# Sliding-window attention in three passes over one Trainium2 core: scores of each half tile of queries against its own 192 keys

## Chip, cores and metric

The kernel runs on one core of one Trainium2 chip. The metric is device time in microseconds (us) of one execution; of several executions the median is taken, and lower is better. All inputs lie in device memory when it starts.

## What is computed

Three stages in a row on 4 sequences of 576 tokens: attention of 8 heads of 64 channels with a window of 128 keys, a mixing of tokens with a channel MLP, and a layer norm with a second channel MLP. The change touches the first stage alone:

```python
scores = scale * np.matmul(q, k.transpose(0, 1, 3, 2))       # 4 x 8 x 576 x 576, 64 channels
rel = pos[:, None] - pos[None, :]
mask = (rel >= 0) & (rel < window)                            # window = 128
scores = np.where(mask, scores + bias[None], -1000000000.0)   # bias = -slope(head) * |rel|
attn = np.exp(scores - np.max(scores, axis=-1, keepdims=True))
attn = attn / (np.sum(attn, axis=-1, keepdims=True) + 1e-09)
return np.matmul(attn, v)
```

A query sees itself and the 127 keys before it. The token mixing is `x + (relu(xT w_tok1) w_tok2)T`, the MLPs are `u + relu(u w_ch1) w_ch2`.

## The kernel before

The 2304 tokens are 18 tiles of 128. One sequence is four and a half tiles, so tile 0 and tile 9 begin a sequence and see their own keys alone; the other 16 tiles see their own 128 keys and the 128 of the tile before.

**Attention of a tile** goes through these steps, in two parts c of four heads each. `load_qk` (L527) fetches the tile's keys into one of the four places of `keys` (a ring), and its queries. `scores` (L591) multiplies, for each of the pairs p of heads, the queries of head j (j = 0, 1) with the keys: 64 channels of head j lie on partitions 64 j to 64 j + 63, so the two heads of a pair take one half of TensorE's rows each. The result `ps_s` has 128 queries on the partitions, and for each j a PSUM bank of its own. For a tile with two key tiles these are 256 columns in fp32. In `softmax`, `copy_predicated` (L626) folds them into 128 columns: column k of the own tile is replaced by column k of the tile before where k lies behind the query (`after` is that mask), since of these two keys the window holds exactly one. Then come a DVE instruction for each head that adds the bias and takes the minimum (L632, on the negated scores), an exponential for each head on ACT (L641), four transposes on TensorE into `ps_t` (L648), a copy out of PSUM (L359) and on POOL two selections (L658) that separate own and previous keys again. `values` (L603) multiplies these with `v`, two heads at once on two halves of TensorE's columns. `normalize` copies the sum out (`ut`, L359), transposes it back (L670) and divides (L372).

**Order of the work.** `packed(i, i2)` records the scores of tile i and the values of tile i - 2 as one block on TensorE: two parts of scores, then two of values. All operations are recorded first with a cost for each engine and a list of what they need, and `Plan.order` then puts them in order for every engine by these costs: what is ready and is due first goes first. The order on an engine is fixed when the program is built. So a changed cost or a new operation can also move operations far from it, and some operations may go to DVE or to POOL (the helpers `minus` L372 and `convert_w`), whichever the plan finds sooner free. The token mixing of earlier tiles (`tok1`, L438 to L440, `tok2`, L728 to L730) is filled in between the attention blocks on TensorE; the conversion of the weights from 64-bit floats goes on beside it on DMA, ACT and DVE (L402 to L429). The MLPs follow: `seven_products` (L987 to L989) and `second` (L1042 to L1044) with DVE adding each result to `u` (L1047).

Of the kernel before, what the change touches and what calls it, by code (L numbers as in the profile page):

```python
# [10 lines left out]
F32 = mybir.dt.float32  # L11
# [39 lines left out]
def batches_of(i):  # L51

    out, t, end = [], i * P, (i + 1) * P
    while t < end:
        b, s = divmod(t, S)
        n = min(end - t, S - s)
        out.append((b, t - i * P, n, s))
        t += n
    return out
# [43 lines left out]
class Plan:  # L103
# [22 lines left out]
    def buf(self, pool, shape, dtype, tag, bufs=1):  # L126
        b = Buf(self, pool, shape, dtype, tag, bufs)
        ring = self.rings.setdefault((pool, tag), [])
        if len(ring) >= bufs:
            b.after = [ring[-bufs]]  # L130
        if ring:
            b.behind = ring[-1]
        ring.append(b)
        return b
# [176 lines left out]
def pe(n):  # L311
    return 2.6 + n / 2.4


def block_kernel(tc, qT, kT, v, wt1, wt2, wa1, wa2, wb1, wb2, g, bias, out):
# [5 lines left out]
    def op(cost, emit, reads=(), writes=(), behind=()):  # L321
        return pl.op(cost, (lambda e: emit()) if len(cost) == 1 else emit, reads, writes, behind)
# [192 lines left out]

    bias_sb = buf("att", [P, 4, H, P], BF16, "bias_sb")

    keys = buf("att", [P, RING, H // 2, P], F32, "keys")
    wt1h, wt1l = ([buf("tok", [P, 5, TOK], F32R, f"wt1{x}{odd}") for odd in range(2)] for x in "hl")
    wt2h = buf("tok", [P, 2, S + P], F32R, "wt2h")  # L520
    wt2l = buf("tok", [P, 2, S + P], F32R, "wt2l")
# [2 lines left out]
    def load_qk(i):  # L524
        r = i % RING
        b = qs[i] = buf("att", [P, H // 2, P], F32, "q", Q_BUFS)
        op({"DMA": 1000}, lambda: nc.sync.dma_start(out=keys.t[:, r].rearrange("p h t -> p (h t)"), in_=kT[i]),  # L527
           writes=[(keys, r)])
        load(b, lambda: b.t.rearrange("p h t -> p (h t)"), P * DM * 4, qT[i])

    def load_v(i):
# [25 lines left out]

    def keys_of(i):

        s = i % RING  # L560
        if starts_batch(i):
            return [i], 0, 0, (s, s + 1, 1)
        table = 3 if len(batches_of(i)) > 1 else 2 if len(batches_of(i - 1)) > 1 else 1
        if s == 0:
            return [i, i - 1], 0, table, (0, RING, RING - 1)
        return [i - 1, i], 1, table, (s - 1, s + 1, 1)

    pv = buf("psb", [P, H // 2, P], F32, "ps_v")
    rs_t, xh_t, xl_t = {}, {}, {}
# [3 lines left out]
    def packed(i, i2):  # L573
# [4 lines left out]

        parts, ready = [], []
        if i is not None:  # L580
            tiles, own, table, (a0, a1, a2) = keys_of(i)
            w = len(tiles) * P
            x = qs[i]
            for c in range(2):
                ps_t[i, c] = buf("psa", [P, 2, 2, 2 * P], F32, "ps_s", 2)

                def scores(c=c, ps=ps_t[i, c]):
                    for p in range(2):
                        for j in range(2):
                            r = slice(j * D, (j + 1) * D)  # L590
                            nc.tensor.matmul(ps.t[:, j, p, :w], x.t[r, 2 * c + p], keys.t[r, a0:a1:a2, 2 * c + p],  # L591
                                             start=True, stop=True)

                parts.append((4 * pe(2 * w), scores, [x] + [(keys, t % RING) for t in tiles], [ps_t[i, c]]))
        if i2 is not None:
            tiles2 = keys_of(i2)[0]
            na = len(tiles2)
# [19 lines left out]

    def softmax(i, c):

        tiles, own, table, _ = keys_of(i)  # L620
        na = len(tiles)
        ps = ps_t[i, c]
        o = slice(own * P, (own + 1) * P)
        if na == 2:
            b = slice((1 - own) * P, (2 - own) * P)
            op({"DVE": 690}, lambda: nc.vector.copy_predicated(  # L626
                ps.t[:, :, :, o], after.t.bitcast(I32).unsqueeze(1).unsqueeze(1).to_broadcast([P, 2, 2, P]),
                ps.t[:, :, :, b]), [ps, after], [ps])
        t = buf("att", [P, 4, P], F32, "t", T_BUFS)
        mn = buf("small", [P, 4], F32, "mn", 3)  # L630
        for m in range(4):
# [569 lines left out]
```

## Time and profile before

| | before |
|---|---|
| median of 3 runs (lowest, highest) | 865.22 us (863.85, 865.59) |
| the profiled execution's own time | 863.28 us |
| its span, first to last instruction | 861.6 us |
| instructions in the profile | 13160 |
| TensorE (PE) busy, share of the span | 834.8 us, 97% |
| VectorE (DVE) | 654.0 us, 76% |
| ScalarE (ACT) | 367.7 us, 43% |
| GpSimd (POOL) | 347.6 us, 40% |
| mean granted clock of TensorE | 0.992 |

A matmul's record reaches from its start to the end that is modelled for it, and records overlap, so a busy share of 97% doesn't say that TensorE streams columns all the time. Where the text speaks of the length of a block of matmuls, it takes the time from the block's first start to the first start of the block behind it. An fp32 matmul of the program leaves two records, so the 8 score matmuls of a tile are 16 records and the 16 value matmuls 32.

### The profile page before, as it was taken

What the parts mean: (1) busy time and instruction counts of PE and PEld (TensorE: products, weight loads), DVE (VectorE), ACT (ScalarE), POOL (GpSimd) and SP (SyncE); (2) the same over time, 40 slices, a digit from 0 to 9 for tenths busy, and PEclk for the clock granted to TensorE, in tenths of its full rate; (3) what the DMA queues carried; (4) which work ended last, traced back from release to release, by engine and by line L of the source; (5) the groups of instructions that cost most, each with busy time, mean ns of one, the idle gap of its engine ahead of it and who ended that gap; (6) DMA issues with size and microseconds to landing.
All of it is one profiled execution on the core that took longest, in us unless ns stands there. A gap on an engine that the chain in (4) does not pass through costs nothing.

```text
span 861.6 us, 13160 instructions
## 1 busy us (share of the span) xinstructions
PE 834.8 (97%) x4478; PEld 688.6 (80%) x4478; DVE 654.0 (76%) x1371; ACT 367.7 (43%) x880; POOL 347.6 (40%) x362
## 2 busy tenths in 40 slices
PE   7999999898999999999997999999999999999997
PEld 6777888676888888788886888888888888888886
DVE  5787676979888889978899956879779755555554
ACT  6888765553344535233355322333354322222221
POOL 2685444555343656522245434534145712221110
PEclk9999999989999999999999999999999999999999
DMA  8588534375778799977861521897377762221112
GB/s 294 184 226 259 186 114 148 110 239 157 246 223 275 265 328 319 355 248 250 279 211 37 194 85 64 257 300 233 126 257 216 242 215 74 74 73 49 49 50 97
DMA packets 73123, 163.92 MB, mean 190 GB/s; under 512 B 8289, under 2 KB 8417, under 8 KB 73057
## 3 DMA queue, kind: packets, MB, share of 16 engines
q1 hardware_dynamic: 72576, 161.78, 56.9%
q0 software_dynamic: 480, 1.31, 0.7%
q8 instruction: 35, 0.57, 0.3%
q14 instruction: 32, 0.25, 0.1%
HBM read 130.55 MB, written 31.20 MB: 188 GB/s over the span
## 4 chain that ended last, share of the span: by engine, by line
PE 65%; DVE 8%; DMA 1%; issue 1%; ACT 0%; SPq 0%; DVEq 0%; ACTq 0%
PE acc L1044 12%; PE acc L1042 12%; PE acc L1043 12%; PE b L987 9%; PE b L989 9%; PE b L988 9%; DVE st L833 2%; DVE u L1047 1%; DVE st L372 1%; PE b L438 1%; PE b L440 1%; PE p L841 1%; PE b L439 1%; DVE hl L920 1%; DVE xl L372 1%
## 5 line engine op out<-in xcount | busy, mean ns | idle before, releaser
L1047 DVE TENSOR_TENSOR u<-acc,u 128x512 f32<-128x512 f32 x252 | 172.3, 686 | 63.5 <-PE acc L1044 60.3
L1042 PE MATMUL acc<-w2h,hh 128*128 128x512 f32 x504 | 198.6, 394 | 2.0 <-DVE u L1047 1.3
L1044 PE MATMUL acc<-w2h,hl 128*128 128x512 f32 x504 | 197.1, 391 | 2.7 <-DVE hl L920 2.6
L1043 PE MATMUL acc<-w2l,hh 128*128 128x512 f32 x504 | 196.9, 391 | 0.0
L918 ACT ACTIVATE hh<-b 128x512 fp32r<-128x512 f32 (+1 forms) x140 | 74.5, 553 | 275.3 <-PE b L989 242.2
L989 PE MATMUL b<-xh,w1l 128*128 128x512 f32 x392 | 154.0, 393 | 2.8 <-DVE w1l L372 2.8
L987 PE MATMUL b<-xh,w1h 128*128 128x512 f32 x392 | 154.3, 394 | 2.2 <-DVE hl L920 1.2
L988 PE MATMUL b<-xl,w1h 128*128 128x512 f32 x392 | 153.5, 392 | 0.0
L920 DVE SCALAR_TENSOR_TENSOR hl<-b,hh 128x512 fp32r<-128x512 f32 (+1 forms) x140 | 85.4, 630 | 59.3 <-ACT hh L918 59.1
L372 POOL TENSOR_TENSOR w1l<-w,w1h 128x512 fp32r<-128x512 f32 (+1 forms) x53 | 68.3, 1289 | 148.9 <-ACT w1h L359 148.6
L1044 PEld LDWEIGHTS acc<-w2h,hl 128*128 128x128 f32 x504 | 94.9, 188 | 23.9 <-DVE hl L920 4.0
L1042 PEld LDWEIGHTS acc<-w2h,hh 128*128 128x128 f32 x504 | 95.2, 189 | 22.9 <-DVE u L1047 3.1
L1043 PEld LDWEIGHTS acc<-w2l,hh 128*128 128x128 f32 x504 | 95.1, 189 | 18.6
L372 POOL TENSOR_TENSOR w1l<-st,w1h 128x512 fp32r<-128x512 f32 x37 | 49.8, 1346 | 113.4 <-ACT w1h L359 102.9
L987 PEld LDWEIGHTS b<-xh,w1h 128*128 128x128 f32 x392 | 74.3, 190 | 18.8 <-DVE hl L920 2.0
L989 PEld LDWEIGHTS b<-xh,w1l 128*128 128x128 f32 x392 | 74.3, 189 | 18.8 <-DVE w1l L372 3.3
L988 PEld LDWEIGHTS b<-xl,w1h 128*128 128x128 f32 x392 | 74.2, 189 | 15.3
L414 ACT ACTIVATE e<-rh 128x512 bf16<-128x512 bf16 (+2 forms) x65 | 41.3, 636 | 65.9 <-DMA rh<-wb 39.8
L641 ACT ACTIVATE pr<-t,mn 128x128 f32<-128x128 f32 x144 | 55.9, 392 | 18.5 <-DVE mn L632 18.5
L658 POOL TENSOR_SCALAR_AFFINE_SELECT pf<-pf 128x512 f32<-128x512 f32 x64 | 42.2, 659 | 34.0 <-ACT pf L359 31.5
L372 DVE TENSOR_TENSOR b<-b,p 128x512 f32<-128x512 f32 x56 | 38.9, 695 | 19.5 <-PE b L989 19.2
L372 POOL TENSOR_TENSOR w2l<-w,w2h 128x512 fp32r<-128x512 f32 x23 | 31.1, 1357 | 47.1 <-ACT w2h L359 46.9
(117 smaller groups left out, 1373.0 us busy)
## 6 DMA issues: line engine op xcount, KB each, us to landing
w<-d SPq DMA_DIRECT2D x85, 256.0 KB, 4.1
rw<-wb SPq DMA_DIRECT2D x32, 512.0 KB, 5.0
rh<-wb SPq DMA_DIRECT2D x32, 512.0 KB, 4.4
rw<-wa SPq DMA_DIRECT2D x24, 512.0 KB, 4.2
rh<-wa SPq DMA_DIRECT2D x24, 512.0 KB, 4.6
d<-y SPq DMA_DIRECT2D x29, 256.0 KB, 4.5
keys<-kT SPq DMA_DIRECT2D x18, 256.0 KB, 4.1
q<-qT SPq DMA_DIRECT2D x18, 256.0 KB, 4.5
```

The costliest lines, as they stand in the source:

```text
L372: pl.op({e: cost[e] for e in on}, lambda e: ENGINE[e].tensor_tensor(get(), ga(), gb(), alu), [*several(a), *several(b), *also], several(dst))
L641: op({"ACT": 580}, lambda m=m: nc.scalar.activation(out=pr.t[:, m], in_=t.t[:, m], func=AF.Exp, bias=mn.t[:, m:m + 1], scale=-1.0, accum_o ...
L658: op({"POOL": 630}, lambda a=a: nc.gpsimd.affine_select(pf.t[:, a], pf.t[:, 1], [[0, 4], [1 - 2 * a, P]], (ALU.is_ge, ALU.is_gt)[a], 0.0, ...
L918: op({"ACT": act(n, True)}, lambda: nc.scalar.activation(out=hh.t[:, c], in_=go(), func=AF.Relu), [o], [(hh, key)])
L920: mark[0] = op({"DVE": dve(n)}, lambda: nc.vector.scalar_tensor_tensor(out=hl.t[:, c], in0=go(), scalar=0.0, in1=hh.t[:, c].bitcast(F32), ...
L987: nc.tensor.matmul(g.t, wh.t[:, w], xh.t, start=start and k == 0, stop=False, skip_group_check=True)
L988: nc.tensor.matmul(g.t, wh.t[:, w], xl.t, start=False, stop=False, skip_group_check=True)
L989: nc.tensor.matmul(g.t, wl.t[:, w], xh.t, start=False, stop=stop and k == 1, skip_group_check=True)
L1042: nc.tensor.matmul(o.t, hh.t[:, c:c + P], wh.t, start=j == 0, stop=False)
L1043: nc.tensor.matmul(o.t, hh.t[:, c:c + P], wl.t, start=False, stop=False)
L1044: nc.tensor.matmul(o.t, hl.t[:, c:c + P], wh.t, start=False, stop=j == 1)
L1047: op({"DVE": dve(DM)}, lambda o=o, i=i: nc.vector.tensor_tensor(u[i].t, o.t, u[i].t, ALU.add), [o], [u[i]])
```

## The change

For tiles with two key tiles, each head's score matmul of 128 queries with 256 keys becomes two matmuls: queries 0 to 63 with keys 0 to 191, queries 64 to 127 with keys 64 to 255. Half q of the queries stands on TensorE's columns 64 q to 64 q + 63 and writes partitions 64 q to 64 q + 63 of `ps_s`, so that two heads and two halves of queries take a quarter of TensorE each. A tile that begins a sequence keeps its form.

So that 192 keys lie in one row, `keys` is now laid out with the tiles side by side in five places, and the keys of every fourth tile (place 4) are loaded a second time into place 0, where the next tile finds them in front of its own; four of the 18 tiles are loaded twice.

`copy_predicated` becomes two: columns 64 to 127 of the own tile on all 128 partitions, and columns 0 to 63 on partitions 0 to 63 (queries 64 to 127 need none there). The own keys now always come last. Costs of the plan: a part of the scores counts 661 ns where it counted 864, and a fold twice 430 where it counted 690.

```diff
@@ -515,7 +515,12 @@
 
     bias_sb = buf("att", [P, 4, H, P], BF16, "bias_sb")
 
-    keys = buf("att", [P, RING, H // 2, P], F32, "keys")
+
+    keys = buf("att", [P, H // 2, (RING + 1) * P], F32, "keys")
+
+    def span(r, h, first, n):
+        return keys.t[r, h, first:first + n]
+
     wt1h, wt1l = ([buf("tok", [P, 5, TOK], F32R, f"wt1{x}{odd}") for odd in range(2)] for x in "hl")
     wt2h = buf("tok", [P, 2, S + P], F32R, "wt2h")
     wt2l = buf("tok", [P, 2, S + P], F32R, "wt2l")
@@ -524,8 +529,10 @@
     def load_qk(i):
         r = i % RING
         b = qs[i] = buf("att", [P, H // 2, P], F32, "q", Q_BUFS)
-        op({"DMA": 1000}, lambda: nc.sync.dma_start(out=keys.t[:, r].rearrange("p h t -> p (h t)"), in_=kT[i]),
-           writes=[(keys, r)])
+        for j in (r + 1, 0) if r == RING - 1 else (r + 1,):
+            op({"DMA": 1000}, lambda j=j: nc.sync.dma_start(out=keys.t[:, :, j * P:(j + 1) * P],
+                                                             in_=kT[i].rearrange("p (h t) -> p h t", t=P)),
+               writes=[(keys, j)])
         load(b, lambda: b.t.rearrange("p h t -> p (h t)"), P * DM * 4, qT[i])
 
     def load_v(i):
@@ -557,13 +564,9 @@
 
     def keys_of(i):
 
-        s = i % RING
         if starts_batch(i):
-            return [i], 0, 0, (s, s + 1, 1)
-        table = 3 if len(batches_of(i)) > 1 else 2 if len(batches_of(i - 1)) > 1 else 1
-        if s == 0:
-            return [i, i - 1], 0, table, (0, RING, RING - 1)
-        return [i - 1, i], 1, table, (s - 1, s + 1, 1)
+            return [i], 0
+        return [i - 1, i], 3 if len(batches_of(i)) > 1 else 2 if len(batches_of(i - 1)) > 1 else 1
 
     pv = buf("psb", [P, H // 2, P], F32, "ps_v")
     rs_t, xh_t, xl_t = {}, {}, {}
@@ -578,20 +581,30 @@
 
         parts, ready = [], []
         if i is not None:
-            tiles, own, table, (a0, a1, a2) = keys_of(i)
-            w = len(tiles) * P
+            tiles, table = keys_of(i)
+            a1 = i % RING + 2
+            a0, w = a1 - len(tiles), len(tiles) * P
             x = qs[i]
             for c in range(2):
                 ps_t[i, c] = buf("psa", [P, 2, 2, 2 * P], F32, "ps_s", 2)
 
                 def scores(c=c, ps=ps_t[i, c]):
                     for p in range(2):
-                        for j in range(2):
-                            r = slice(j * D, (j + 1) * D)
-                            nc.tensor.matmul(ps.t[:, j, p, :w], x.t[r, 2 * c + p], keys.t[r, a0:a1:a2, 2 * c + p],
-                                             start=True, stop=True)
-
-                parts.append((4 * pe(2 * w), scores, [x] + [(keys, t % RING) for t in tiles], [ps_t[i, c]]))
+                        if len(tiles) == 1:
+                            for j in range(2):
+                                r = slice(j * D, (j + 1) * D)
+                                nc.tensor.matmul(ps.t[:, j, p, :w], x.t[r, 2 * c + p], span(r, 2 * c + p, a0 * P, w),
+                                                 start=True, stop=True)
+                            continue
+
+                        for q in range(2):
+                            for j in range(2):
+                                r, m = slice(j * D, (j + 1) * D), slice(q * D, (q + 1) * D)
+                                nc.tensor.matmul(ps.t[m, j, p, q * D:q * D + 3 * D], x.t[r, 2 * c + p, m],
+                                                 span(r, 2 * c + p, a0 * P + q * D, 3 * D), start=True, stop=True)
+
+                parts.append((4 * pe(3 * D if w > P else P) * (2 if w > P else 1), scores,
+                              [x] + [(keys, k) for k in range(a0, a1)], [ps_t[i, c]]))
         if i2 is not None:
             tiles2 = keys_of(i2)[0]
             na = len(tiles2)
@@ -617,15 +630,18 @@
 
     def softmax(i, c):
 
-        tiles, own, table, _ = keys_of(i)
+        tiles, table = keys_of(i)
         na = len(tiles)
+        own = na - 1
         ps = ps_t[i, c]
         o = slice(own * P, (own + 1) * P)
         if na == 2:
-            b = slice((1 - own) * P, (2 - own) * P)
-            op({"DVE": 690}, lambda: nc.vector.copy_predicated(
-                ps.t[:, :, :, o], after.t.bitcast(I32).unsqueeze(1).unsqueeze(1).to_broadcast([P, 2, 2, P]),
-                ps.t[:, :, :, b]), [ps, after], [ps])
+
+            for rows, c0 in ((P, D), (D, 0)):
+                op({"DVE": 430}, lambda rows=rows, c0=c0: nc.vector.copy_predicated(
+                    ps.t[:rows, :, :, P + c0:P + c0 + D],
+                    after.t[:rows, c0:c0 + D].bitcast(I32).unsqueeze(1).unsqueeze(1).to_broadcast([rows, 2, 2, D]),
+                    ps.t[:rows, :, :, c0:c0 + D]), [ps, after], [ps])
         t = buf("att", [P, 4, P], F32, "t", T_BUFS)
         mn = buf("small", [P, 4], F32, "mn", 3)
         for m in range(4):
```

**What moves.** On TensorE, around the scores of tile 6 (`ps_s` scores, `ps_v` values and, with `ut`, their transposes back, `ps_t` the transposes of the softmax, `tok` the token mixing), before:

```order
L591 MATMUL ps_s<-keys,q 128x256 x8
L603 MATMUL ps_v<-pf,v 64x128 x16
L648 MATMUL ps_t<-ident,pr 128x128 x4
L670 MATMUL ps_v<-ident,ut 128x128 x4
L438 MATMUL tok<-xh,wt1h_381 128x512
L439 MATMUL tok<-xl,wt1h_381 128x512
L440 MATMUL tok<-xh,wt1l_402 128x512
L648 MATMUL ps_t<-ident,pr 128x128 x4
```

and with the change:

```order
L603 MATMUL ps_s<-keys,q 64x192 x16
L616 MATMUL ps_v<-pf,v 64x128 x16
L664 MATMUL ps_t<-ident,pr 128x128 x4
L686 MATMUL ps_v<-ident,ut 128x128 x4
L664 MATMUL ps_t<-ident,pr 128x128 x4
L438 MATMUL tok<-xh,wt1h_419 128x512
L439 MATMUL tok<-xl,wt1h_419 128x512
L440 MATMUL tok<-xh,wt1l_432 128x512
```

The scores are 16 matmuls where they were 8, and the second four transposes of the softmax stand ahead of the three matmuls of the token mixing that they stood behind; it is so at tile 4 too.

On DVE, the fold of tile 3, both parts, with what follows it, before:

```order
L626 COPY_PREDICATED ps_s<-after,ps_s 128x4x128 x2
L632 ISA t,mn<-ps_s,bias_sb 128x128
L632 ISA mn 128x1
```

and with the change:

```order
L641 COPY_PREDICATED ps_s<-after,ps_s 128x4x64 x2
L641 COPY_PREDICATED ps_s<-after,ps_s 64x4x64 x2
L648 ISA t,mn<-ps_s,bias_sb 128x128
L648 ISA mn 128x1
```

The two large pieces, one of each part, go first and the two small ones behind them, all four ahead of the first bias instruction.

On SyncE, whose queue issues the loads in this order, the first loads of keys, queries and values, before:

```order
L527 DMA keys<-kT 128x512
L351 DMA v<-v 128x512
L351 DMA q<-qT 128x512
L351 DMA v<-v 128x512
L760 DMA bias_sb<-bias 128x2048
L402 DMA rh<-wt 128x2048
L527 DMA keys<-kT 128x512
```

and with the change:

```order
L533 DMA keys<-kT 128x4x128
L351 DMA v<-v 128x512
L351 DMA q<-qT 128x512
L533 DMA keys<-kT 128x4x128
L351 DMA v<-v 128x512
L776 DMA bias_sb<-bias 128x2048
L533 DMA keys<-kT 128x4x128
```

The first row is tile 3 into place 4, the fourth is the same tile into place 0; each load is now written in pieces of 128 elements. In the stages behind, the kinds and numbers of instructions are the same on TensorE and ACT, some transposes of `u` stand some tens of rows further ahead, and of the low parts `w1l` (128x512) of the weights 34 stand on DVE where 27 stood, the others on POOL.

## Rows read from the trace of the kernel before

**Rows 1.** The page's first part, and of the second the granted clock

```profile
span 861.6 us, 13160 instructions
PE 834.8 (97%) x4478; PEld 688.6 (80%) x4478; DVE 654.0 (76%) x1371; ACT 367.7 (43%) x880; POOL 347.6 (40%) x362
PEclk9999999989999999999999999999999999999999
```

**Rows 2.** Stretches: length, busy time by engine (instructions), granted clock, DMA share, GB/s

```profile
0.00:20.00 20.00, 15.12 (x112) 12.19 (x114) 10.48 (x60) 13.60 (x55) 5.07 (x19) 0.97 0.86 303
20.00:82.00 62.00, 60.32 (x569) 46.77 (x567) 47.98 (x216) 53.45 (x198) 41.61 (x62) 0.98 0.76 219
82.00:147.00 65.00, 65.00 (x560) 53.55 (x560) 44.78 (x162) 43.59 (x142) 32.09 (x45) 1.00 0.47 153
147.00:180.00 33.00, 28.64 (x126) 22.87 (x125) 31.42 (x44) 17.70 (x32) 16.89 (x13) 0.90 0.42 132
180.00:862.00 682.00, 665.70 (x3119) 553.24 (x3117) 519.35 (x893) 239.39 (x457) 251.97 (x223) 1.00 0.57 191
```

**Rows 3.** PE in order of time: start, length of the group, line, shape, records

```profile
41.52 2.00 PE L591 MATMUL ps_s<-keys,q 64*128 64x256 f32 x16
43.45 1.97 PE L603 MATMUL ps_v<-pf,v 128*64 128x128 f32 x32
45.35 0.66 PE L648 MATMUL ps_t<-ident,pr 128*128 128x128 f32 x4
46.12 0.66 PE L670 MATMUL ps_v<-ident,ut 128*128 128x128 f32 x4
46.53 0.47 PE L438 MATMUL tok<-xh,wt1h 128*128 128x512 f32 x1
...
47.30 0.60 PE L648 MATMUL ps_t<-ident,pr 128*128 128x128 f32 x4
```

**Rows 4.** PE in order of time, tile 9, which has one key tile

```profile
63.03 1.16 PE L591 MATMUL ps_s<-keys,q 64*128 64x128 f32 x16
64.12 0.33 PE L603 MATMUL ps_v<-pf,v 128*64 128x128 f32 x2
```

**Rows 5.** PE and its weight loads to 145 us, by shape: busy, mean ns of one

```profile
L591 PE MATMUL ps_s<-keys,q 64*128 64x256 f32 x256 | 33.4, 402 | 0.7 <-DMA q<-qT 0.7
L603 PEld LDWEIGHTS ps_v<-pf,v 128*64 128x64 f32 x522 | 28.1, 137 | 5.8 <-issue 2.3 <-POOL pf L658 1.3 <-DVE ps_s L626 1.0
L591 PEld LDWEIGHTS ps_s<-keys,q 64*128 64x128 f32 x288 | 26.5, 194 | 7.1 <-issue 3.0 <-DVE mn L632 1.0 <-DVE m L421 0.2
```

**Rows 6.** PE in order of time, first and last of six score blocks from 81.95 us

```profile
81.95 2.00 PE L591 MATMUL ps_s<-keys,q 64*128 64x256 f32 x16
...
125.69 2.00 PE L591 MATMUL ps_s<-keys,q 64*128 64x256 f32 x16
```

**Rows 7.** DVE to 145 us, by shape: busy, mean ns of one

```profile
L626 DVE COPY_PREDICATED ps_s<-after,ps_s 128x512 f32<-128x512 int32 x32 | 22.1, 695 | 11.5 <-PE ps_s L591 10.8 <-issue 0.6
L429 DVE SCALAR_TENSOR_TENSOR w<-m,s 128x512 f32<-128x512 uint32 x5 | 4.1, 824 | 0.0
L429 DVE SCALAR_TENSOR_TENSOR y<-m,s 128x256 f32<-128x256 uint32 x5 | 2.1, 425 | 0.2
```

**Rows 8.** PE in order of time, the first blocks and tile 8's exponentials

```profile
7.38 2.00 PE L591 MATMUL ps_s<-keys,q 64*128 64x256 f32 x16 [0.70 <-DMA q<-qT]
...
61.62 1.47 PE L648 MATMUL ps_t<-ident,pr 128*128 128x128 f32 x4
```

**Rows 9.** ACT between 41 and 48 us, in order of time

```profile
45.47 0.60 ACT L359 ACTIVATE ut<-ps_v 128x512 f32<-128x512 f32 x1 [0.41 <-PE ps_v L603]
46.10 0.60 ACT L359 ACTIVATE pf<-ps_t 128x512 f32<-128x512 f32 x1
```

**Rows 10.** The page's DMA part: the hardware queue, and the keys' loads

```profile
q1 hardware_dynamic: 72576, 161.78, 56.9%
...
keys<-kT SPq DMA_DIRECT2D x18, 256.0 KB, 4.1
```

**Rows 11.** PE where the MLP begins

```profile
170.23 0.40 PE L988 MATMUL b<-xl,w1h 128*128 128x512 f32 x1
173.45 0.80 PE L989 MATMUL b<-xh,w1l 128*128 128x512 f32 x1 [2.82 <-DVE w1l L372]
174.04 0.63 PE L987 MATMUL b<-xh,w1h 128*128 128x512 f32 x1
```

## The prediction

> **What bounds the kernel now.** I read the page's busy shares first, then the stretches, then TensorE in order of time around one attention tile, then DVE's and ACT's rows for the steps between. TensorE is busy 97% of the span at full clock [rows 1], but its records overlap, so the stretches have to say where it really sets the pace [rows 2]. The attention lies in the first 147 us. From 0 to 20 us TensorE is busy 15.12 of 20: the start is a chain of loads, softmax steps and transposes. From 20 to 82 us it is busy 60.32 of 62, with ACT close behind at 53.45. From 82 to 147 us it is busy 65.00 of 65, with DVE at 44.78 and ACT at 43.59: here TensorE is the bound and nothing else is near. From 147 to 180 us DVE is the tight one (31.42 of 33). So a shorter block on TensorE counts in full from 82 to 147 us, partly from 20 to 82, and hardly before 20.
>
> **The score block.** In tile 6 the scores start at 41.52 and the values behind them at 43.45, so a block of 16 records takes 1.93 us [rows 3]. Sixteen records of 0.402 us each make 6.4 us, which do not fit in 1.93 one after the other [rows 5]: the two heads of a pair run side by side, in 8 steps of two. Tile 9 has the same 16 records with 128 columns and takes 64.12 - 63.03 = 1.09 us [rows 4]. The difference, 0.84 us, is 8 steps times 128 columns, so 128 columns cost 0.105 us a step, and 1.93 - 8 x 0.21 = 0.25 us is fixed (first weights, last results, change to the next form). The value block, 32 records, takes 45.35 - 43.45 = 1.90 us, in 16 steps of two halves of TensorE's columns, so halves by columns run side by side as well as halves by rows [rows 3].
>
> The change makes 16 matmuls of 192 columns, 32 records. If four quarters run side by side these are 8 steps of 0.1575 us: 1.26 + 0.25 = 1.51 us, a gain of 0.42. A weight load of 64 columns takes 137 ns where one of 128 takes 194 [rows 5], and the first load of a block is not hidden, which gives up to 0.05 more. **I take 0.45 us a block**; there are 16 such blocks. No row shows four quarters at once, so the bounds are wide. Best: 0.47. Middle: records that cannot follow each other faster than in the value block, (1.90 - 0.25) / 32 = 0.052 us, make 1.90 us, a gain of 0.03. Worst: only two quarters at a time, 16 steps of 0.1575 + 0.25 = 2.77 us, a loss of 0.84. I take the good end, because rows and columns each already run in pairs, and because in both pair forms the step is what its columns need (16 steps of 0.105 and 0.25 make 1.93 for the value block, which takes 1.90).
>
> The Trainium skill, "TensorE: Matmul & The Clock Gate", section "Wait — 56ns, not 53.3ns?", speaks against the change: with hardware decode off, the sequencer spends about 62 ns on each matmul, and that binds once the array's work per matmul is shorter. By it 32 records would be an estimated 1.98 us and the gain gone. The trace does not agree as it stands: the value block's records follow at 0.052 us.
>
> **What of it counts.** From 82 to 147 us there are six blocks, the first at 81.95, the last at 125.69 [rows 6], and TensorE never idles: 6 x 0.45 = 2.7 us.
>
> From 20 to 82 us there are seven (tiles 4 to 8, 10, 11; 3.15 us). Without them ACT would be busy 53.45 of 58.85 us, 91%, and TensorE would meet it more often. One block buys nothing: behind tile 8's scores four transposes take 1.47 us, one exponential after another [rows 8]. Two give part of it back through the new order: at tiles 4 and 6 the second transposes now stand ahead of the token mixing. Their PSUM tile comes free when ACT has copied it, from 46.10 to 46.70; they would be due at 46.53, where the mixing starts now [rows 3, 9]; that is a wait of about 0.25 each. So 6 x 0.45 - 2 x 0.25 = 2.2 us.
>
> Before 20 us there are three (tiles 1 to 3), in a chain. There a part's scores are ready 4 steps x 0.05 = 0.2 us sooner, but the folds take longer (next): minus 0.1 each, 0.3 in all.
>
> **The folds.** One copy of 512 columns is 695 ns, 32 of them. A 256-column one is bounded below by half, 348, and above by what another DVE instruction of 256 columns takes beside one of 512: 425 against 824 [rows 7]. I take 430, as the nearer in shape; that 64 partitions take as long as 128 is assumed. Two are 860: plus 165 ns a part (0 to 0.17), 5.3 us of DVE in all. Both parts' folds stand ahead of the first bias instruction, so the first part waits 0.33 us more, which is the chain's loss above. As load it hides: DVE is idle 14 us between 20 and 82 and 20 us between 82 and 147 [rows 2].
>
> **The loads.** All traffic of that queue, 161.78 MB in 56.9% of the span, comes to 0.79 us of all 16 DMA engines for 256 KB [rows 10]. Four more loads are 3.2 us of them, with the engines idle a quarter of the time from 20 to 82 us [rows 2]. Keys are fetched three tiles, over 20 us, ahead, against 4.1 us to land, so this is hidden, except at the start, where TensorE already waits 0.70 us for a load [rows 8]. Pieces of a quarter of the size may slow those first loads: bounds nothing and one more load's 0.79 us; I take 0.2, the nearer to nothing since the amount of data is the same.
>
> **The MLPs.** What is computed there is unchanged. At the entry TensorE waits 2.82 us for DVE's part of a weight, and the matmuls after it take 0.63 us where the last before it took 0.40, with a granted clock of 0.90 in that stretch [rows 2, 11]; this sequence follows the last token mixing and moves with it. Seven more 512-column subtractions on DVE and a few transposes ahead of their old place: I put that at nothing, plus or minus 2 us, because a stall like the one above can shrink or grow.
>
> **Sum.** 2.7 + 2.2 - 0.3 - 0.2 = 4.4 us. The profiled execution took 863.28 us; 4.4 off is 858.9. The median of the runs was 865.22, 1.94 above it, so **the median after is 860.8 us**.
>
> **Rivals.** *No gain per block* (the change doesn't do what it says): records stay at 0.052 us, 16 x 0.03 = 0.5 us gained, 0.5 lost at the start: 865.2 us. For it: no row shows records closer. Against it: within a step two records start together, so the pace seen is what columns need.
>
> *Two quarters at a time*: the third quarter shares its row half with the first and its column half with the fourth, and must wait until one of them is done. It decides as soon as a block of scores takes longer than 1.93 us; at 2.77 the kernel loses 16 x 0.84 = 13.4 us: 878.6 us, slower. Against it: column halves do share the rows in the value block. For it: nothing shows both splits at once. A rule of the Trainium skill on that page, section "Part 3: Packing small matmuls — row/col tiling", points this way: weight loads overlap with running matmuls only when the row group differs. By it two quarters of one row half would not overlap; the trace does not agree, since in the value block loads and matmuls of the same rows overlap.
>
> *The softmax chain takes over* from 20 to 82 us: with 0.33 us more of folds per tile and ACT at 91%, none of the 2.2 us arrives and only 2.7 - 0.5 remains: 863.0 us. For it: ACT is the second engine there. Against it: the listed idle time is small.
>
> *The MLPs' new order* costs 3 us, one more stall as at 173 us: 863.8 us.
>
> **How the numbers follow.** Forecast 0.58; no gain 0.12; two at a time 0.09; chain 0.13; order 0.08. A measurement of this kernel tells about 0.2%, 1.7 us, from no change. Faster by more: the forecast, two thirds of the chain and a third of the order, 0.69. Within: 0.17. Slower: two at a time, and a quarter of no gain and order together, 0.14. The range goes from all 16 blocks at 0.47 (7.5 us) with 1 us from the MLPs, 856.7, to no gain with 1.5 us lost in the MLPs, 866.7; it leaves out two at a time and about a tenth more.
>
> **What would show it.** Right: score blocks of about 1.5 us from first start to the values; folds near 430 ns; TensorE's stretch from tile 12 to tile 17 shorter by 0.45 us a tile; the MLPs as long as before. Wrong: a block of 1.9 or 2.8 us; new idle time of TensorE on ACT's exponentials between 20 and 82 us; tile 1's block later than 7.38 us by more than 0.5; or an attention shorter by 4 us and a total that is not.

## The result: 871.5 us, 0.8% slower, and the profile after

| | before (same chip) | after |
|---|---|---|
| median (lowest, highest) | 864.62 us (863.85, 865.59) | 871.52 us (868.58, 872.62) |
| ratio, 95% interval | | 1.0076 [1.0059, 1.0093] |
| span of the profiled execution | 861.6 us | 869.3 us |
| first product of the MLP | 169.89 us | 180.78 us |

The forecast was 860.8 us, range 856.7 to 866.7. The page of after, which answers to [rows 1]:

```profile
span 869.3 us, 13706 instructions
PE 832.9 (96%) x4734; PEld 686.1 (79%) x4734; DVE 658.0 (76%) x1407; ACT 366.0 (42%) x880; POOL 343.1 (39%) x358
PEclk8898999999999999999999999999999999999999
```

TensorE is busy 1.9 us less, and the span is 7.7 us longer, so TensorE idles 9.6 us more. The clock row (the share of TensorE's full clock that was granted, in tenths) and the stretches, beside [rows 2], say where:

```profile
0.00:20.00 20.00, 12.87 (x128) 10.44 (x128) 7.88 (x52) 8.91 (x36) 2.46 (x15) 0.89 0.88 286
20.00:82.00 62.00, 53.73 (x598) 41.28 (x598) 41.98 (x194) 48.05 (x178) 38.84 (x60) 0.87 0.76 203
82.00:147.00 65.00, 64.14 (x697) 52.00 (x695) 48.91 (x207) 47.46 (x170) 33.91 (x47) 1.00 0.49 157
```

Up to 82 us every engine is busy for less time than before and the granted clock is down to 0.87 to 0.89 (before 0.97 and 0.98); from there to 147 us it is 1.00 again.

**The score block does what it should.** TensorE in order of time, tile 6 of after, beside [rows 3], and the groups to 145 us, beside [rows 5, 7]:

```profile
46.90 1.53 PE L603 MATMUL ps_s<-keys,q 64*64 64x192 f32 x32
48.36 1.97 PE L616 MATMUL ps_v<-pf,v 128*64 128x128 f32 x32
50.26 0.66 PE L664 MATMUL ps_t<-ident,pr 128*128 128x128 f32 x4
```

```profile
L641 DVE COPY_PREDICATED ps_s<-after,ps_s 128x256 f32<-128x256 int32 x32 | 13.6, 428 | 10.6 <-PE ps_s L603 8.0 <-POOL rc L690 2.2
L641 DVE COPY_PREDICATED ps_s<-after,ps_s 64x256 f32<-64x256 int32 x32 | 12.0, 415 | 0.0
```

The block takes 48.36 - 46.90 = 1.46 us where it took 1.93: 0.47 less. The 32 records start in eight groups of four, the four within 20 ns, so four quarters do run side by side. The folds are 428 and 415 ns.

**Where 7.7 us went.** I cut both traces at first starts of score blocks. Before they are tile 4 at 27.20, tile 8 at 56.05, tile 10 at 68.87, tile 12 at 81.95 and tile 17 at 125.69 [rows 6]; after 33.21, 60.36, 80.53, 93.83 and 135.37.

| | before | after | difference |
|---|---|---|---|
| start to tile 4 | 27.20 | 33.21 | +6.0 |
| tile 4 to 8 | 28.85 | 27.15 | -1.7 |
| tile 8 to 10 | 12.82 | 20.17 | +7.4 |
| tile 10 to 12 | 13.08 | 13.30 | +0.2 |
| tile 12 to 17 | 43.74 | 41.54 | -2.2 |
| tile 17 to the MLP | 44.20 | 45.41 | +1.2 |
| MLP to the end | 691.7 | 688.5 | -3.2 |

Four and five blocks of 0.43 and 0.44 us are gained from tile 4 to 8 and from tile 12 to 17, where TensorE idles little. Two other places lose three times as much. TensorE and ACT in order of time at the first place:

```profile
8.96 2.84 PE L603 MATMUL ps_s<-keys,q 64*64 64x192 f32 x32 [2.11 <-DMA q<-qT]
...
21.27 1.11 PE L686 MATMUL ps_v<-ident,ut 128*128 128x128 f32 x4 [4.19 <-ACT ut L359]
```

```profile
20.30 0.43 ACT L414 ACTIVATE e<-rh 128x256 bf16<-128x256 bf16 x1 [3.39 <-DMA rh<-wt]
20.63 0.58 ACT L359 ACTIVATE ut<-ps_v 128x512 f32<-128x512 f32 x1
```

TensorE waits 4.19 us for `ut`, a copy of values that were there by 16.5 us. But on ACT `ut` stands behind `e`, the first step of a weight's conversion, and that waits 3.39 us for `rh`, the weight's load. At the second place, from tile 8 to tile 10, it is the same twice:

```profile
64.95 0.46 ACT L414 ACTIVATE e<-rh 128x288 bf16<-128x288 bf16 x1 [2.74 <-DMA rh<-wt]
...
75.20 0.47 ACT L414 ACTIVATE e<-rh 128x288 bf16<-128x288 bf16 x1 [3.69 <-DMA rh<-wt]
```

```profile
66.43 0.71 PE L686 MATMUL ps_v<-ident,ut 128*128 128x128 f32 x4 [2.06 <-ACT ut L359]
...
78.80 0.65 PE L686 MATMUL ps_v<-ident,ut 128*128 128x128 f32 x4 [2.82 <-ACT ut L359]
```

The stretch from tile 8 to tile 10, first before, then after:

```profile
56.05:68.87 12.82, 12.06 (x128) 9.66 (x127) 10.76 (x47) 11.69 (x46) 10.53 (x17) 1.00 1.08 263
```

```profile
60.36:80.53 20.17, 14.54 (x148) 11.22 (x147) 11.18 (x54) 13.23 (x51) 12.23 (x20) 0.83 1.04 247
```

TensorE idles 5.6 us there where it idled 0.8, and its busy time is 2.5 us longer at a granted clock of 0.83. The DMA engines have no idle share in this stretch (1.08 and 1.04), before the change or after it.

ACT's waits up to 85 us, first line before, second after:

```profile
ACT e L414 <- DMA rh<-wt: 1.4, 2, 1.1
```

```profile
ACT e L414 <- DMA rh<-wt: 9.8, 3, 3.7
```

Why `rh` is late at the start stands on the queue of SyncE (SP), which issues nearly all loads one after another. First before, then after, in order of time:

```profile
8.53 0.33 SPq L760 DMA_DIRECT2D bias_sb<-bias  x1
9.19 0.33 SPq L402 DMA_DIRECT2D rh<-wt  x1
9.92 0.33 SPq L527 DMA_DIRECT2D keys<-kT  x1
10.55 0.33 SPq L351 DMA_DIRECT2D q<-qT  x1
```

```profile
8.84 0.55 SPq L533 DMA_DIRECT2D keys<-kT  x1
10.13 0.33 SPq L351 DMA_DIRECT2D v<-v  x1
11.04 0.33 SPq L776 DMA_DIRECT2D bias_sb<-bias  x1
11.85 0.55 SPq L533 DMA_DIRECT2D keys<-kT  x1
12.44 0.62 SPq L351 DMA_DIRECT2D q<-qT  x1
13.29 0.33 SPq L402 DMA_DIRECT2D rh<-wt  x1
```

The load at 8.84 is the second one of tile 3's keys, which is new. Counted from the start, `rh` was the 15th load of the queue and is now the 18th: the second load and, by the plan's new order, the keys and queries of the tile behind it stand ahead. It is issued 4.1 us later and `e` runs 5.1 us later (15.23 before). Each keys load also holds the queue for 0.55 us where it took 0.33. At the second place the queue is not what delays `rh`: it issues the load at 65.43 as soon as the `e` at 64.95 is done with the one before, and the load then takes 9.7 us to land.

### The profile page after: what moved, and what is told of

Same layout as the page of the kernel before. It is cut to its first block, busy times and chain, and to the rows that moved or that the text cites. A ratio compares the mean times of both kernels' runs of the same rounds, so it can differ in the third digit from the quotient of the medians.

```text
span 869.3 us, 13706 instructions
## 1 busy us (share of the span) xinstructions
PE 832.9 (96%) x4734; PEld 686.1 (79%) x4734; DVE 658.0 (76%) x1407; ACT 366.0 (42%) x880; POOL 343.1 (39%) x358
## 4 chain that ended last, share of the span: by engine, by line
PE 68%; DVE 5%; issue 1%; ACT 1%; DVEq 0%; ACTq 0%
PE acc L1060 12%; PE acc L1058 12%; PE acc L1059 12%; PE b L1003 9%; PE b L1005 9%; PE b L1004 9%; DVE st L849 2%; PE b L438 1%; PE b L440 1%; PE b L439 1%; PE p L857 1%; DVE st L372 1%; DVE u L1063 1%; DVE hl L936 0%; DVE xl L372 0%
## 5 line engine op out<-in xcount | busy, mean ns | idle before, releaser
L372 POOL TENSOR_TENSOR w1l<-w,w1h 128x512 fp32r<-128x512 f32 (+1 forms) x51 | 64.8, 1271 | 137.7 <-ACT w1h L359 137.3
L372 POOL TENSOR_TENSOR w1l<-st,w1h 128x512 fp32r<-128x512 f32 x35 | 47.6, 1361 | 111.6 <-ACT w1h L359 102.0
L372 POOL TENSOR_TENSOR st<-w 128x256 f32<-128x256 f32 x44 | 36.7, 849 | 42.6 <-DMA w<-d 19.5
```

The lines of the kernel that those rows point to most:

```text
L372: pl.op({e: cost[e] for e in on}, lambda e: ENGINE[e].tensor_tensor(get(), ga(), gb(), alu), [*several(a), *several(b), *also], several(dst))
```

## The experiments

All ratios are to the kernel before on the same chip. e3, e6 and e13 leave out most or all of the earlier keys at tiles 4, 8, 12 and 16, so they compute something else. A difference between two rows is known to some 0.2 to 0.3%, about 2 us: one under 2 us is not clear of noise.

| run | what it is | median us | ratio [95%] |
|---|---|---|---|
| e1 | the loads alone | 872.73 | 1.0102 [1.0077, 1.0128] |
| e2 | the folds alone | 864.84 | 1.0011 [0.9998, 1.0025] |
| e3 | no second loads | 867.71 | 1.0036 [1.0015, 1.0058] |
| e4 | 2048-byte pieces | 868.05 | 1.0046 [1.0032, 1.0060] |
| e5 | the plan's old costs | 870.20 | 1.0070 [1.0048, 1.0091] |
| e6 | e4 without second loads | 863.26 | 0.9988 [0.9972, 1.0005] |
| e7, e12 | ring of nine, 2048-byte pieces | 858.86, 858.94 | 0.9942 [0.9917, 0.9966], 0.9944 [0.9926, 0.9963] |
| e8 | e7, old costs | 863.66 | 0.9994 [0.9976, 1.0011] |
| e9 | e7 with 256-wide scores, old costs | 866.47 | 1.0027 [1.0009, 1.0046] |
| e10 | e7 with 512-byte pieces | 862.84 | 0.9992 [0.9981, 1.0004] |
| e11 | keys in GpSimd's queue | 868.39 | 1.0063 [1.0042, 1.0085] |
| e13 | e4, second loads of 8 rows | 866.34 | 1.0033 [1.0022, 1.0044] |
| e14 | e12 with 256-wide scores, same order | 863.19 | 0.9993 [0.9978, 1.0007] |
| e15 | the change with 256-wide scores, same order | 876.00 | 1.0131 [1.0105, 1.0157] |
| e16 | one weight load moved ahead | 866.97 | 1.0042 [1.0024, 1.0061] |
| e17 | e16, second loads behind weights | 866.34 | 1.0025 [1.0011, 1.0040] |
| e18 | e17 with 2048-byte pieces | 862.58 | 0.9988 [0.9974, 1.0002] |

My theory after the trace was: the change's **loads** make the weights late. The rival: the plan's **order**, new for its changed costs, sets ACT to wait.

**Parts alone.** e1 gives the kernel before only the new layout of `keys` with its second loads; e2 only the two-piece fold.

> The loads of the change alone (keys side by side, every fourth tile loaded twice, pieces of 512 bytes), with the scores and the fold as before. Theory (loads): the added and cut-up loads delay the weight loads behind them on SyncE's queue, ACT waits for these in order, TensorE idles behind ACT. Then this alone loses what the changed kernel lost before the scores gave anything back, 6 to 14 us: 870 to 878 us, and ACT waits over 5 us for weight loads before 82 us. Rival (folds): 864 to 866 us, ACT's waits as before. Rival (order: the plan's new costs move ACT's work to a bad place): 864 to 867 us, since scores and folds keep their old costs here.

> The kernel before with the fold in two pieces. Theory (loads): DVE hides it, 864 to 866.5 us. Rival (folds): the longer softmax chain costs 0.33 us in each of 16 tiles and more at the start, 868 to 871 us.

The loads alone lose 0.0102 x 864 = 8.8 us, more than the whole change; the folds 1 us (2.2 at most by the interval). In e1 tile 4 starts 6.7 us late, at 33.87, behind one wait for `rh` of 5.5 us. From tile 8 to tile 10 it loses nothing:

```profile
62.44:75.24 12.80, 12.04 (x127) 9.65 (x126) 10.75 (x47) 11.67 (x46) 10.50 (x17) 1.00 1.17 227
```

So these loads, in e1's own order of the work, spoil the first place and not the second.

**What of the loads.** e3 drops the second loads, e4 has the host put the keys of half a tile side by side, e6 is both.

```diff
e3: -        for j in (r + 1, 0) if r == RING - 1 else (r + 1,):
e3: +        for j in (r + 1,):
e4: -    keys = buf("att", [P, H // 2, (RING + 1) * P], F32, "keys")
e4: +    keys = buf("att", [P, (RING + 1) * 2, H // 2, D], F32, "keys")
```

> The changed kernel without the four second loads: place 0 is set to zero once at the start, so the tiles 4, 8, 12 and 16 see zeros in place of the keys of the tile before. Theory (loads), if the second loads are the harm: 858 to 863 us, and TensorE's waits on ACT at tiles 3 and 8 to 9 shrink below 2 us each. If the cutting into pieces is the harm: 868 to 871 us. Rivals (folds, order): 868 to 872 us.

> The changed kernel with keys laid out by half tiles, the heads inside, so that each load is 2048 bytes a partition again (the host arranges the keys so); the second loads stay. A score matmul then reads three stretches of 64 columns. Theory (loads), if the pieces are the harm: 858 to 863 us; if the second loads are: 867 to 871 us. The length of a score block, 1.46 us, should stay if three stretches stream as one.

> The changed kernel with whole pieces of 2048 bytes and without the second loads (place 0 set to zero once, so tiles 4, 8, 12 and 16 see zeros for the tile before): both harms of the loads off, the new order on. Theory (two harms): tile 4 starts at 27 us or before, the stretch from tile 8 to 10 stays near 20 us: 862 to 867 us. Rival (loads alone): 856 to 860 us.

Each helps by 2.6 to 3.5 us and both by 7.6, which brings the time back to that of the kernel before. e4 has the change's order on every engine, so its 2.6 us belong to the pieces: in the trace of after, to 85 us, a 512-byte packet takes 30 ns on the mean, four of them 120, and one of 2048 bytes 104. e3 and e6 keep the change's order on TensorE, ACT and DVE too; on SyncE's queue the four second loads are gone and the first `rh` stands in place 15 again. So what they gain belongs to the second loads, their transfers and the places that they take together. With whole pieces these are worth 5.0 us (1.0046 to 0.9988).

**The order.** e5 is the change with other costs in the plan: a part's scores count what they did before, a fold 345.

```diff
-                parts.append((4 * pe(3 * D if w > P else P) * (2 if w > P else 1), scores,
+                parts.append((4 * pe(2 * w), scores,
```

> The changed kernel with the plan's costs of before (a part of the scores 864 ns, the two folds 345 each), so that the order on the engines is nearly that of before; loads, scores and folds are the changed ones. Theory (two harms: the loads at the start, about 6 us by tile 4; the plan's order at tiles 8 to 10, about 7 us, where ACT stands waiting for weight loads): the second goes, the first stays: 862 to 867 us, and from tile 8's scores to tile 10's 12 to 14 us where the changed kernel took 20. Rival (loads alone): 869 to 873 us.

The plan's costs are not it: the time stays, and most of the loss between tiles 8 and 10 (18.1 us) does. e5's order is still not that of before, so this does not clear the order.

**Another queue.** e11 issues the keys on GpSimd (`nc.gpsimd.dma_start` for `nc.sync.dma_start` in `load_qk`), with the order of TensorE, ACT and DVE unchanged.

> The changed kernel with its 22 loads of keys issued by GpSimd instead of SyncE, all else as it is: the same bytes, the same pieces, the same waits for places, in another queue. Queue theory (the loads of the weights stand behind the keys' on SyncE): ScalarE's waits for rh fall from 9.8 us before 85 us to 3 to 5, tiles 8 to 10 take 13 to 15 us for 20.2, and the time falls to 862 to 866 us, as far as GpSimd's own work isn't held up by its waits for places. Transfer theory (the DMA engines are short of time, whichever queue the keys are in): waits and time stay within 2 us of the changed kernel, 869 to 873 us, or rise, since packets of GpSimd's queue take longer.

ACT's waits up to 85 us:

```profile
ACT e L414 <- DMA rh<-wt: 2.9, 4, 1.3
```

As the queue theory wants, the waits fall to 2.9 us, and tiles 8 to 10 take 15.5 for 20.2. The time missed its range and is only 1.1 us shorter than after's, which is not clear of noise: the first keys come later in this queue (tile 0's scores start at 7.9 us for 5.7), and tiles 4 to 8 take 29.4 us for 27.2. The Trainium skill, "DMA: Bandwidth & Descriptors", section "Issuing engines are not separate DMA queues", says that all queues share the same 16 DMA engines and that another issuer saves only the time to issue, usually small. The time of this run (1.1 us) does not speak against it; ACT's waits do, which are 6.9 us shorter. One doubt stays: GpSimd's queue packs the same keys into packets of 4096 bytes, so not the queue alone has changed.

**Place on the queue.** e13 keeps e4's order and lets the second loads carry 8 of 128 rows. e16 moves one load on SyncE's queue, the first `rh`, to place 13, and changes nothing else on any engine; e17 also puts the other three second loads behind the next `rh`; e18 adds the pieces of e4.

```diff
-        for k in self.order():
+        ks = self.order()
+        head = min(self.heads, key=ks.index)
+        ks.remove(head)
+        ks.insert(ks.index(min(self.second, key=ks.index)), head)
+        for k in ks:
```

> The changed kernel with half-tile pieces as before (four places), and the four second loads carry 8 of 128 partitions, in the same place of every engine's order. Tiles 4, 8, 12 and 16 see zeros, set at the start, for most of the previous tile's keys: that part of the computation is left out. Beside the same kernel with whole second loads (868.05 us, 1.0046) only 1 MB of transfers is gone. Volume theory (the second loads take time of the DMA engines that the weights behind them need): 863 to 866 us, ScalarE's waits for rh 5 us for 9.3. If the gain of 4 to 5 us seen without the second loads came from the other order that the plan then gave: 867 to 869 us, waits 8 us or more.

> The changed kernel with one load moved in SyncE's order, and nothing else on any engine: the first rh<-wt, which stands 18th there (15th before the change), goes ahead of the first second load, to place 13. Place theory (what counts is how many loads stand ahead of the weight's on SyncE's queue): it is issued near 8 us for 13.29, ScalarE's wait of 3.39 us at 20.30 is gone, tile 4's scores start at 28 to 30 us for 33.2, and the time falls by 3 to 5 us to 866.5 to 868.5. Transfer theory (the DMA engines are full at the start, and what is loaded sooner makes another load late): the wait moves to the loads of the keys or q, and the time stays at 870 to 873 us.

> As the run before, and the other three second loads go behind the next rh<-wt on SyncE's queue (one to two places each). Place theory: the two waits between 60 and 82 us (2.74 and 3.69) shrink too, by 0.6 us for the issue that no longer stands ahead and up to 0.8 us of transfer each: 1 to 2 us more than the run before, 865 to 867.5 us. If only the start counts: the same as the run before.

> The run before with keys by half tiles in 2048-byte pieces, in the same order of all engines: all that the change's loads cost is taken back, but for 1 MB of second loads and the plan's order of the rest. If place and pieces together are the loss: the pieces give 2.6 to 4.1 us more, as in the three pairs of the same order, 862 to 865 us, at or under the kernel before. If an order that is worse on other engines is the rest: 865 to 867 us.

The bytes of the second loads are worth 1.1 us (1.0046 to 1.0033), not clear of noise, and ACT still waits 8.9 us; e13's time fell between its two ranges. One load moved gives 2.9 us; it now stands two places ahead of its place before the change, so part of this may be more than the change had cost. SyncE's queue and TensorE in e16:

```profile
8.19 0.33 SPq L356 DMA_DIRECT2D q<-qT  x1
8.76 0.39 SPq L407 DMA_DIRECT2D rh<-wt  x1
10.13 0.55 SPq L541 DMA_DIRECT2D keys<-kT  x1
```

```profile
25.09 1.12 PE L694 MATMUL ps_v<-ident,ut 128*128 128x128 f32 x4 [1.86 <-ACT ut L364]
...
28.65 1.53 PE L611 MATMUL ps_s<-keys,q 64*64 64x192 f32 x32
```

The load is issued at 8.76 for 13.29, the first `e` runs at 15.38 without a wait, tile 4 starts at 28.65 for 33.21, and the MLP 4.7 us sooner. The second `e` now waits instead, 2.4 us. e17's time is 1.5 us less again (1.0042 to 1.0025), which is not clear of noise, and the waits that it was to shorten did not shrink: between 60 and 82 us ACT waits 5.17 and 1.78 us for `rh`, in e16 3.07 and 3.16. The pieces then give 3.2 (to 0.9988). From the change to e18 this makes 7.6 us, and the time is that of the kernel before.

It is not so at both places. First starts of score blocks, each from one profiled execution, in us:

| run | start to tile 4 | tile 8 to 10 |
|---|---|---|
| before | 27.20 | 12.82 |
| after | 33.21 | 20.17 |
| e1 | 33.87 | 12.80 |
| e3 | 29.68 | 20.49 |
| e4 | 29.90 | 20.42 |
| e6 | 26.00 | 17.45 |
| e11 | 30.71 | 15.53 |
| e13 | 30.87 | 17.18 |
| e16 | 28.65 | 19.97 |
| e17 | 28.32 | 21.06 |
| e18 | 26.27 | 16.51 |

At the start place and pieces are the whole loss: e18 and e6 are there a little sooner than before. From tile 8 to tile 10 neither place (e16, e17) nor pieces (e4) nor the second loads (e3) alone shorten the stretch; whole pieces without the second loads (e6) or with them behind the weights (e18) take back 2.7 and 3.7 us of 7.4, and the keys in another queue (e11) 4.6. The rest, 2.7 to 4.6 us, stays in these runs, which have the change's order on TensorE, ACT and DVE. It is not there in e1, which has the change's loads in another order. e6, tile 8 to tile 10:

```profile
53.17:70.62 17.45, 13.90 (x147) 10.66 (x146) 11.73 (x54) 13.23 (x51) 12.06 (x20) 0.90 0.98 263
```

**A ring of nine places.** Tile 9 sees no tile before it, so with nine places no tile stands in front of place 0's and no second load is needed: e7, complete.

```diff
-RING = 4
+RING = 9
...
-            a1 = i % RING + 2
+            a1 = i % RING + 1
```

> The changed kernel with nine places for keys in place of five, whole pieces and no second loads: tile 9 begins a sequence, so no tile needs the keys of the last place beside the first. Complete, plan's new costs. Theory (two harms): as the run without second loads, 862 to 867 us. Rival (loads alone): 856 to 860 us.

> The ring of nine with whole pieces and with the plan's costs of before: both harms off. Theory (two harms): 856 to 861 us, faster than both kernels, since 0.46 us a tile from tile 3 on remain. Rival (the faster scores are worth nothing because something else bounds the attention): 863 to 866 us.

> The changed kernel with nine places and no second loads, but its 512-byte pieces: loads that never wait for a place, in small pieces. Pieces alone cost 3.5 to 4 us in the ring of four (the step from the changed kernel to the one with whole pieces). If the pieces cost because the SyncE queue, already late with waits for places, issues and moves them longer, then without the waits most of that cost goes: 859 to 861 us. If the cost lies in the DMA engines themselves (24 ns more per packet of a 2-KB row), it stays whole: 862 to 864 us.

> The ring of nine with quarters, half-tile pieces and no second loads once more, beside the two above on one chip: 857 to 861 us as before (ratio 0.992 to 0.997) if the gain over the kernel before holds; the difference to the kernel with 256-wide scores is what the quarters are worth once their loads cost nothing, the difference to the one with 512-byte pieces what the pieces cost once no load waits.

It beats both kernels, twice: 858.9 us. The stretches of e12:

```profile
0.00:20.00 20.00, 16.33 (x182) 12.55 (x184) 9.23 (x60) 14.20 (x58) 5.60 (x20) 1.00 0.90 320
20.00:82.00 62.00, 55.03 (x702) 43.78 (x698) 50.12 (x236) 53.06 (x198) 41.45 (x64) 1.00 0.80 234
```

TensorE keeps its full clock, ACT waits 2.4 us for `rh`, and tile 17's scores start at 121.6 us for 125.69 [rows 6]. e10 has e12's order and 512-byte pieces: 4.1 us for these alone. That fits the packets: 18 loads of 512 small ones at 31 ns (e10) are 286 us, of 128 large ones at 99 ns (e12) 228; the 58 us between are 3.6 of all 16 engines. The Trainium skill, "DMA: Bandwidth & Descriptors", section "Specifications", has 512 bytes as the least for line rate; the trace does not agree to the full, since here the same 2048 bytes take 124 ns in four pieces and 99 in one. e8 shows what the plan's order can do by itself: only costs differ from e7, and 4.5 us are gone.

**The quarters alone.** e9, e14 and e15 take the quarters out: scores of 256 keys again, in e14 and e15 with the same order on all engines.

> The ring of nine places in half-tile pieces and no second loads, but scores of 256 keys, one fold and the plan's costs of the kernel before: the loads cured, without the quarters. If the quarters are worth what their blocks show (0.47 us in each tile, so 2.7 us from the six blocks between 82 and 147 us and up to 2.5 before) and the ring cures only what the change's loads spoilt, this stands at the kernel before or up to 0.3% under it, 862 to 865 us, and 3 to 6 us over the ring of nine with quarters. If instead the ring is what gains and the quarters give nothing, it stands at the ring of nine with quarters, 857 to 861 us.

> The ring of nine with half-tile pieces and two-piece folds, in exactly its order on all engines, but the scores as matmuls of 256 keys for two quarters of TensorE, as before the change: the quarters alone undone. Each of 16 blocks is 0.47 us longer. If a block counts in full where TensorE is the bound (5 blocks after 82 us, 2.3 us) and mostly before it: 863 to 866 us, 4 to 7 us over the 858.9 of the ring of nine with quarters. If the distance to the earlier run with 256-wide scores (866.5) came mainly from its other order: 860 to 862 us.

> The changed kernel, its loads and its order on all engines, with the scores as matmuls of 256 keys for two quarters: the quarters alone undone, amid late loads. Where TensorE waits for the loads of the weights anyway, a shorter block buys nothing: the five blocks after tile 12 and the four from tile 4 to tile 8 count (9 x 0.45 = 4 us), the others don't: 874 to 877 us. If no block counts: 871 to 873 us.

With the order held the quarters are worth 4.2 us in the ring of nine (0.9993 to 0.9944) and 4.8 in the change (1.0131 to 1.0076), each give or take 2 to 3; the prediction's sum has 4.4. e9 alone would have said 7.2: its one-piece fold and its other order together cost 3 us more.

## Why the prediction was wrong

- **The score block** was right: 0.47 us where I took 0.45, four quarters at once. "Two quarters at a time" and "no gain" fell.
- **What of it counts** was right: from tile 12 to tile 17 2.2 us for five blocks; e14 and e15 give 4.2 and 4.8 us in all, for 4.4 in the sum. It asked what the new order does to TensorE only at tiles 4 and 6; the stretch from tile 8 to tile 10, where it saw nothing gained or lost, lost 7.4 us.
- **The folds** were right: 428 and 415 ns, and hidden as far as e2 can tell (0 to 2 us).
- **The MLPs** came 3.2 us shorter in the profiled execution, for 0 plus or minus 2. At the entry TensorE waits 1.53 us for DVE's part of a weight, 1.3 less than in [rows 11]; e12 and e14, with and without quarters in one order, have 689.2 and 689.5 us there, and e9 in another order 692.4, so this follows the order and not the quarters.

TensorE in order of time, after, at the MLP's entry:

```profile
183.03 0.80 PE L1005 MATMUL b<-xh,w1l 128*128 128x512 f32 x1 [1.53 <-DVE w1l L372]
```

- **"The loads" is the step that failed.** "So this is hidden, except at the start", I wrote, and took 0.2 us; the runs show 7.6 us (1.0076 to 0.9988, e6 and e18). Three things in it were wrong. First, I asked whether the keys themselves come in time, not who stands behind the new loads on SyncE's queue. There the first weight load went from the 15th to the 18th place, ACT waits for it in order, `ut` stands behind on ACT, and TensorE waits for `ut`: moving that one load ahead gives 2.9 us (e16), leaving out the second loads 3.5 (e3). Second, the pieces were bounded by "nothing and one more load's 0.79 us", for the first loads alone: with the order held they cost 2.6 (e4), 3.2 (e18) and 4.1 us (e10), and at the first loads alone TensorE's wait grew by 1.4 us, 2.11 for 0.70. Tile 1's block starts at 8.96 us for 7.38, which the prediction itself had named as a sign of being wrong. Third, "the engines idle a quarter of the time from 20 to 82 us" is a mean: from tile 8 to tile 10 their share was 1.08 before the change. No rival of the prediction had this mechanism.
- **The softmax chain rival** named the right sign to look for, TensorE idle on ACT, but for DVE's folds; the cause is a load.
- **Left open**: quarters -4.5 and mended loads +7.6 make +3.1, the change measured +6.6. So the kernel of after loses some 3.5 us more than these loads. The traces have as much between tile 8 and tile 10, where e6 and e18 still take 4.6 and 3.7 us longer than before. The second loads' bytes are not it (e6 has none), the folds are 0 to 2 us (e2), and the order of the work differs from before's; since e1 loses nothing there, the order is the likely cause, but it was not tried apart. What the ring of nine gains beyond e18 (3.8 us) is not split either: it has no second loads, freer places and another order.

## What to carry to other kernels

Cost a new or larger load by what stands behind it on its issuing queue, not only by whether it lands in time itself: list that queue's order before and after, and follow each load that moved back to the engine that waits for it in order and to what is queued there. Where a schedule is computed from costs, undo one part with the order held, since other costs in the plan alone moved this kernel by 4.5 us (e8). And keep the bytes of a row in one piece: let the host arrange them.

## What I had not expected

- Four 64 x 64 quarters take 32 fp32 records in 1.46 us where two column halves need 1.90 for 32 [rows 3]; with the 0.25 us that the prediction estimates for start and end taken off, 0.038 us a record for 0.052.
- From about 8 us on a keys load holds SyncE's issue for 0.55 us with 512-byte pieces, 0.33 with 2048 (before, e4).
- Between 60 and 75 us one weight load took 9.7 us to land, and before another one of that size 4.3 in the same stretch. GpSimd's own loads ran beside both, with 480 packets in after and 240 before; whether they are the cause is not shown. First after, then before:

```profile
rh<-wt SPq DMA_DIRECT2D x1, 288.0 KB, 9.7
```

```profile
rh<-wt SPq DMA_DIRECT2D x1, 288.0 KB, 4.3
```

- The granted clock did not follow the last wait alone. In after TensorE waits 2.11 us before tile 1's scores and the block runs at a granted clock of 0.50 (1.2 of 2.4 GHz), 2.77 us; in e16 it waits 2.42 us at the same place and the block runs at 1.00, 1.47 us. The stretch of the block, first after, then e16 (the clock is the third number from the end):

```profile
8.96:11.73 2.77, 2.77 (x32) 1.96 (x33) 0.85 (x2) 1.18 (x7) 0.24 (x1) 0.50 1.08 376
```

```profile
8.87:10.34 1.47, 1.47 (x33) 1.19 (x33) 0.44 (x2) 1.47 (x9) 0.00 (x0) 1.00 1.03 357
```

What made the difference is open; TensorE's work ahead of it was the same in both (17 records in the 3.2 and 3.5 us from tile 0's scores on).
